# A new opening for a fused attention and MLP kernel: fewer warming products, another load order, another hand-written order up to the table

## The chip, the cores and the metric

The kernel runs on one core of one Trainium2 chip. The metric is device time in microseconds (us) of one execution, as the median of several runs. Five engines work beside each other and wait for one another by semaphores: PE (TensorE, matrix products into PSUM), DVE (VectorE), ACT (ScalarE), POOL (GpSimd) and SP (SyncE, which here only issues DMAs). ACT and POOL issue a few DMAs as well.

## The reference

One sequence of 2048 rows with 576 features goes through a linear-attention block with 32 heads of 18 features and then through an MLP with 4608 hidden units.

```python
qkv = layernorm(x) @ wqkv                 # q, k, v: 32 heads of 18
pq, pk = q @ w_phi, k @ w_phi             # per head, 18 x 18
phi_q = concat(softmax(pq), softmax(-pq)) # 36 features per head
phi_k = concat(softmax(pk), softmax(-pk))
kv  = sum over rows of phi_k * v          # one table per head
z   = sum over rows of phi_k
o   = (phi_q @ kv) / (phi_q @ z + 1e-6)
h   = x + o @ wo
out = h + gelu(layernorm(layernorm(h)) @ w1 + b1) @ w2 + b2
```

No query row can be finished before the table kv has seen all 2048 key rows. So the opening has to produce all keys, values and the table before the first row can go on to the MLP.

## The kernel before, in words

The 2048 rows stand as 16 tiles of 128 partitions, taken in 8 pairs p = 0 to 7. The order of all instructions on all engines is written out by hand: the body ends in a long list of calls, one per step, and each engine carries out its share of the list in that order. A step therefore waits for its own inputs and for whatever stands ahead of it on its engine.

The opening, up to the table, has these parts (lines of the kernel before):

- **Weights.** `warm` (L243) runs products of the identity on PE. `load_wk` (L153) brings the key part of wqkv, `flip_mm`/`flip_ev` (L359, L366) transpose its five chunks on PE and copy them with ACT. w_phi is loaded by two DMAs on POOL (L179, L182) and spread by `spread` (L215) into a block-diagonal form, in five groups on POOL. `fold_k_mm`/`fold_k_ev` (L372, L384) multiply the two into nine blocks of a folded key weight `wkp`. For the queries `load_wq` (L593), `turn_wq` (a DMA transpose, L369) and `fold_mm`/`fold_ev` (L387, L401) do the same later; `swap_q` (L405) copies halves of that weight by DMA.
- **Rows.** `load_x` (L172) brings x; the first two tiles come by ACT's queue (L176). `stats` (L272) takes mean and variance on DVE, `power` (L282) the reciprocal roots on POOL, `scale` (L304) normalises on DVE, or on ACT after `centre` (L297) has made a shift on POOL. A normalised pair is transposed by PE (`turn_x_mm`, `turn_x_ev`, pairs 0 and 1) or by a DMA transpose (`turn_dma`, L318, all other pairs).
- **Products.** `key_mm` and `value_mm` (18 matmuls each, L452 and L427, all by `project` at L416) for each pair and half i of the features; `key_exp` (L455) takes two exponentials on ACT, `value_ev` (L431) copies values with ACT. `key_sum` (L487, on DVE) adds up the softmax sums and takes reciprocals, `key_weigh` (L490) multiplies them in, on POOL but for the last. `query_mm`, `query_exp`, `query_sum`, `query_weigh` do the same for queries.
- **Table.** `sums` (L550) accumulates the table of one tile in the PSUM tile `acc_kv`; `table` (L565) masks it into SBUF. Then `combine_mm` (L627) and `divide` (L648) make attention rows and the MLP begins.

`load_values` (L163) brings the value weights `wv`, as four DMAs: upper half of the partitions by POOL, lower half by SP. PSUM tiles of PE's results in the opening come from one pool, `two`, with three slots (L109), so a product waits until the result three places before it has been copied out. The helper `double_bank` and the tail after the table use the same pool.

Each DMA issued by SP or ACT reuses one of eight semaphore lanes in turn, so an issue waits until the one eight places before it has landed.

## Time and profile before

| | |
|---|---|
| median of 3 runs | 392.47 us (392.47 to 392.67) |
| the profiled execution | 392.93 us |
| span of its trace, first to last instruction | 391.2 us |
| granted TensorE clock | 1.00 |
| read from HBM, written | 17.20 MB, 2.36 MB |

The page of the profile gives busy time by engine, the busy share of forty equal slices of the span, DMA queues, and the chain of work that ended last, followed back from the last instruction. PEld is the load of weights into the array, which overlaps PE. In the timeline a row is: start, duration, engine, line, operation, output<-inputs, count, and in brackets how long the engine had been idle and what released it. A row of several instructions spans them all. An engine with q behind its name is its instruction queue, for example while it issues a DMA. A group row gives busy time and mean ns of one. A DMA row gives size and the median time from issue to landing.

### The profile page before, as it was taken

To read this page: it belongs to the slowest core of one execution; us is meant where nothing else is said; L and a number is where in the kernel's file an instruction comes from. 1 tells how busy PE (TensorE), PEld (TensorE's weight loads), DVE (VectorE), ACT (ScalarE), POOL (GpSimd) and SP (SyncE) were. 2 spreads that over 40 slices of the span, in tenths; PEclk is the share of its full clock that TensorE was granted. 3 is DMA by queue.
4 is the path that set the end of the run, shared out by engine and by line. 5 is a ranking of instruction groups with operands and counts; after the bars stand their busy time and mean duration, and the time that the engine had idled before them with its cause. 6 is when DMAs were issued, how large, how long until landed. Compare 5 with 4: busy or idle time off the path is not lost.

```text
span 391.2 us, 10237 instructions
## 1 busy us (share of the span) xinstructions
PE 382.1 (98%) x4492; PEld 267.4 (68%) x4493; DVE 163.0 (42%) x367; ACT 165.0 (42%) x293; POOL 119.5 (31%) x154
## 2 busy tenths in 40 slices
PE   7899999999999999999999999999999999999997
PEld 3677877779978887844457887444677864447773
DVE  5899778495248388590029322000470000000100
ACT  4988888578501850056650000666300026661000
POOL 6479798215504564144003111000031110000120
PEclk9999999999999999999999999999999999999999
DMA  8999796999555466723005543000051000000000
GB/s 232 212 165 193 161 200 128 216 313 267 176 106 107 91 107 134 107 61 61 0 2 63 90 106 50 14 1 2 2 112 40 17 17 0 2 2 0 17 32 15
DMA packets 74140, 35.43 MB, mean 91 GB/s; under 512 B 62514, under 2 KB 71296, under 8 KB 73968
## 3 DMA queue, kind: packets, MB, share of 16 engines
q1 hardware_dynamic: 73232, 32.47, 41.0%
q0 software_dynamic: 576, 2.01, 2.2%
q8 instruction: 35, 0.57, 0.6%
q10 hardware_dynamic: 288, 0.30, 0.2%
q14 instruction: 9, 0.07, 0.1%
HBM read 17.20 MB, written 2.36 MB: 50 GB/s over the span
## 4 chain that ended last, share of the span: by engine, by line
PE 89%; DMA 4%; DVE 4%; POOL 1%; issue 1%; ACT 1%; POOLq 0%; DVEq 0%
PE po L1183 36%; PE ph L1139 36%; PE pk L422 6%; PE pa L690 5%; PE pv L422 3%; DMA home<-shared 3%; DMA w<-in_A_w_phi_dram 1%; PE pn L641 1%; DVE st L277 1%; PE acc_kv L558 1%; DVE shared L312 1%; DVE ob L655 0%; POOL w L217 0%; PE pW L392 0%; DVE sk L473 0%
## 5 line engine op out<-in xcount | busy, mean ns | idle before, releaser
L1161 ACT ACTIVATE home<-ph,b1col 128x512 bf16<-128x512 f32 (+1 forms) x180 | 98.5, 599 | 169.3 <-PE ph L1139 165.6
L1183 PE MATMUL po<-w,home 128*128 128x288 bf16 (+2 forms) x1151 | 143.2, 286 | 0.1
L1139 PE MATMUL ph<-shared,w 64*128 64x512 bf16 (+2 forms) x1638 | 141.3, 331 | 0.4 <-DVE shared L341 0.4
L1183 PEld LDWEIGHTS <-home 128*128 128x128 bf16 x1152 | 109.3, 98 | 32.2 <-issue 1.8
L1139 PEld LDWEIGHTS <-w 64*128 64x128 bf16 x1638 | 80.2, 94 | 60.4 <-issue 1.3
L1187 DVE TENSOR_TENSOR ot<-po,hb 128x288 bf16<-128x288 f32 (+2 forms) x32 | 14.4, 452 | 106.7 <-PE po L1183 97.1
L1172 POOL TENSOR_TENSOR hb<-xh,b2bc 128x576 f32<-128x576 bf16 x16 | 20.4, 1275 | 104.5 <-DVE ot L1187 103.0
L422 PEld LDWEIGHTS <-home 64*128 64x128 bf16 x864 | 42.5, 94 | 12.5 <-DMA home<-shared 1.9
L508 POOL TENSOR_TENSOR padded<-home,rq 128x540 bf16<-128x540 bf16 x32 | 34.9, 1103 | 37.2 <-DVE rq L500 15.4
L699 DVE TENSOR_TENSOR xh<-pa,xh 128x288 bf16<-128x288 f32 x32 | 13.1, 448 | 70.8 <-PE pa L690 70.8
L253 POOL TENSOR_TENSOR rs<-va,mhalf 128x1 f32<-128x1 f32 x16 | 8.8, 552 | 104.1 <-DVE va L251 104.1
L479 POOL TENSOR_TENSOR phik<-phik,rk 128x576 bf16<-128x576 bf16 x31 | 35.7, 1181 | 4.0 <-DVE rk L475 2.6
L473 DVE TENSOR_REDUCE sk<-phik 128x64 f32<-128x1152 bf16 x16 | 21.2, 1327 | 4.8 <-ACT phik L444 4.8
L444 ACT ACTIVATE home<-pk 128x576 bf16<-128x576 f32 x32 | 18.9, 653 | 8.8 <-PE pk L422 6.7
L499 DVE TENSOR_REDUCE sk<-home 128x64 f32<-128x1152 bf16 x16 | 21.0, 1313 | 0.0
L422 PE MATMUL pk<-shared,home 64*128 64x288 bf16 x288 | 19.3, 283 | 1.1 <-DMA home<-shared 1.0
L444 ACT ACTIVATE phik<-pk 128x576 bf16<-128x576 f32 x32 | 18.5, 650 | 3.5 <-PE pk L422 3.5
L422 PE MATMUL pv<-wv,home 64*128 64x288 bf16 x288 | 19.7, 283 | 0.2 <-DMA wv<-in_A_wqkv_dram 0.2
L422 PE MATMUL pk<-wqp,home 64*128 64x288 bf16 x288 | 19.7, 283 | 0.2 <-ACT home L444 0.2
L654 DVE RECIPROCAL rec<-pn 128x18 f32<-128x18 f32 (+1 forms) x32 | 8.0, 249 | 28.3 <-PE pn L641 28.3
L690 PE MATMUL pa<-wo,shared 64*128 64x288 bf16 x288 | 18.8, 283 | 0.0
L690 PEld LDWEIGHTS <-shared 64*128 64x128 bf16 x288 | 13.9, 94 | 4.3 <-issue 0.5
(80 smaller groups left out, 202.4 us busy)
## 6 DMA issues: line engine op xcount, KB each, us to landing
w<-in_B_w_dram SPq DMA_DIRECT2D x21, 432.0 KB, 8.3
out_dram<-ot SPq DMA_DIRECT2D x15, 144.0 KB, 1.9
xh<-in_A_x_dram SPq DMA_DIRECT2D x3, 576.0 KB, 10.8
wo<-in_A_wo_dram SPq DMA_DIRECT2D x2, 648.0 KB, 6.7
w<-in_B_w_dram POOLq DMA_DIRECT2D x3, 432.0 KB, 10.1
w<-in_A_wqkv_dram SPq DMA_DIRECT2D x4, 157.5 KB, 9.6
w<-in_A_wqkv_dram SPq DMA_DIRECT2D x2, 288.0 KB, 4.7
wqp<-wqp SPq DMA_DIRECT2D x2, 288.0 KB, 3.5
```

What stands on the lines that cost most here:

```text
L422: nc.tensor.matmul(dst[:, a, 0 : hi - lo], lhs[rows, c, :], w[rows, slot, lo:hi], start=(n == 0), stop=(n == KC - 1),)
L444: nc.scalar.activation(rows[:, :, i * HH : (i + 1) * HH, s, :], flight[key, p, i][:, :, 0:HALF].rearrange("p a (h f) -> p a h f", f=DH), A ...
L473: nc.vector.tensor_reduce(sk[:, :, :], part_of(dst, i), AX.X, ALU.add)
L479: eng.tensor_tensor(part, part, flight["r" + key, p, i][:, a, :].rearrange("p (h o) -> p h o", o=1).to_broadcast([P, NH, DH]), ALU.mult,)
L499: nc.vector.tensor_reduce(sk[:, :, :], part_of(phiq[p], i), AX.X, ALU.add)
L508: eng.tensor_tensor(padded[:, a, g0 * P : (g0 + 5) * P].rearrange("p (g k) -> p g k", k=P)[:, :, 0:STEP].rearrange("p g (h f) -> p g h f", ...
L690: nc.tensor.matmul(pa[a], oT[p % 2][rows, c, :], wo[rows, c, cs], start=(c == 0), stop=(c == KC - 1),)
L1139: nc.tensor.matmul(ph[half][:, lo:hi], w1[p_ // 9][rows, c, p_ % 9 * P : (p_ % 9 + 1) * P], ln2T[rows, c, base + lo : base + hi], start=(c ...
L1161: nc.scalar.activation(hidden(m), ph[half][:, 0:width], AF.Gelu_apprx_tanh, bias=b1col[:, m : m + 1], scale=1.0,)
L1172: nc.gpsimd.tensor_tensor(hb[:, :], xh[:, t, :], b2bc[:, :], ALU.add)
L1183: nc.tensor.matmul(po[:, :], hidden(m)[:, i_ * P : (i_ + 1) * P], w2[m // 18][:, m % 18, cs], start=(j == 0), stop=(j == NM - 1),)
L1187: nc.vector.tensor_tensor(ot[:, cs], po[:, :], hb[:, cs], ALU.add)
```

## The change

Six things change.

1. `warm(13)` becomes `warm(10)`.
2. The small part of w_phi (72 rows) is loaded by ACT's queue instead of POOL's.
3. The first key product, `key_mm(0, 0)`, goes through the nine blocks of the contraction in the order in which they were folded (5, 4, 3, 8, 0, 6, 1, 7, 2) instead of 0 to 8.
4. `power(2)` and `power(3)` take two rows of roots each; before, `power(2)` took all four of pairs 2 and 3.
5. `acc_kv` is zeroed by a memset on DVE instead of an activation on ACT, and the ones column of `vals` is set by a call in the list, `ones()`, instead of at the start.
6. The list of steps up to the table is in a new order, and after the table the remaining query products are in another order.

In the new list several `scale` change engine (nine are on ACT instead of five); `load_values` on SP and the two last `load_x` stand ahead of all `load_wq`; the fold order is new; six products instead of seven stand ahead of `key_mm(2, 0)`; three `key_weigh` instead of one are on DVE.

```diff
     for t in range(2):
         nc.scalar.dma_start(xh[:, t, :], x_v[:, t, :])
+    nc.scalar.dma_start(wph[0:72, 4, :], wphi_rows[504:576, :])
...
-    nc.gpsimd.dma_start(wph[0:72, 4, :], wphi_rows[504:576, :])
...
-    nc.scalar.activation(
-        acc_kv[:, :, :].rearrange("p b (r f) -> p (b r) f", f=P),
-        ident[:, :].rearrange("p (o f) -> p o f", o=1).to_broadcast([P, 8, P]),
-        AF.Copy, scale=0.0,
-    )
-    nc.vector.memset(vals[:, :, :, DH], 1.0)
-
-    def spread(g):
+    nc.vector.memset(acc_kv[:, :, :], 0.0)
+
+    def ones():
+        nc.vector.memset(vals[:, :, :, DH], 1.0)
+
+    def spread(g, eng=nc.gpsimd):
...
     def power(p):
-        n = 2 if p < 2 else 4
+        n = 2 if p < 4 else 4
...
+    fold_order = []
+
...
     def fold_k_ev(c, copy):
+        fold_order.append(c)
         copy(wkp[:, c, :], folded_whole("k", c, P))
...
     def key_mm(p, i):
-        features("k", wkp, p, i, PLAIN)
+        features("k", wkp, p, i, PLAIN if p or i else [(c, c) for c in fold_order])
```

The list before, up to `key_mm(2, 0)`, several calls to a line:

```python
warm(13); load_values(1, 1, pool); load_values(0, 1, pool); load_wk(2); load_wk(1); load_wk(0)
load_x(2, 4); load_x(4, 8); spread(4); flip_mm(4); flip_ev(4, act); stats(0, 0); spread(0)
flip_mm(2); flip_mm(3); flip_ev(2, act); flip_mm(1); flip_ev(3, act); flip_ev(1, act)
flip_mm(0); flip_ev(0, act); spread(1); spread(3); spread(2)
fold_k 3, 8, 4; load_wq(4); stats(0, 1); power(0); fold_k 5; load_wq(1); load_x(8, 12); load_wq(3)
stats(1, 0); fold_k 1, 7; stats(1, 1); scale(0, 0, vec); fold_k_mm(0); window_masks()
load_values(0); fold_k_ev(0, act); load_values(1); power(1); centre(1, 1); fold_k_mm(6)
stats(2, 0); fold_k_ev(6, act); scale(0, 1, vec); scale(1, 1, act); turn_x_mm(0); stats(2, 1)
scale(1, 0, vec); stats(3, 0); turn_x_ev(0, 0, act); load_wq(0); turn_x_ev(0, 1, dve)
stats(3, 1); stats(4, 0); fold_k_mm(2); fold_k_ev(2, act); turn_x_mm(1); stats(4, 1); power(2)
centre(3, 1); scale(2, 1, vec); turn_x_ev(1, 0, act); scale(2, 0, vec); stats(5, 0); load_biases()
stats(5, 1); power(4); key_mm(0, 0); turn_x_ev(1, 1, act); key_mm(0, 1); key_mm(1, 0)
key_exp(0, 0); key_exp(0, 1); centre(4, 1); key_exp(1, 0); value_mm(1, 0); value_mm(1, 1)
value_ev(1, 0, act); value_ev(1, 1, act); turn_wq(1); load_wq(2); turn_dma(2); scale(3, 1, act)
key_mm(1, 1); key_exp(1, 1); turn_wq(0); key_sum(0, 1); key_weigh(0, 1, 1, pool)
key_weigh(0, 1, 0, pool); scale(3, 0, vec); value_mm(0, 0); value_ev(0, 0, act); key_mm(2, 0)
...
```

The list after, up to the same step:

```python
load_wk(1); load_wk(2); load_values(0, 1, pool); load_values(1, 1, pool); warm(10); spread(2, pool)
stats(0, 0); spread(1, pool); flip_mm(4); flip_mm(2); load_wk(0); flip_mm(0); load_x(2, 4)
flip_ev(4, act); flip_ev(2, act); load_x(4, 8); flip_ev(0, act); flip_mm(1); flip_ev(1, act)
stats(0, 1); stats(1, 0); spread(4, pool); spread(0, pool); flip_mm(3); flip_ev(3, act)
spread(3, pool); fold_k 5, 4; fold_k_mm(3); load_values(0); power(0); fold_k_ev(3, act); fold_k 8
load_values(1); load_x(8, 12); fold_k 0; stats(1, 1); scale(0, 0, vec); power(1); fold_k 6
load_x(12, 16); fold_k_mm(1); load_wq(4); stats(2, 0); fold_k_ev(1, act); scale(0, 1, vec)
stats(2, 1); turn_x_mm(0); turn_x_ev(0, 0, act); fold_k 7; scale(1, 1, vec); stats(3, 0)
turn_x_ev(0, 1, dve); load_wq(2); scale(1, 0, vec); fold_k_mm(2); stats(3, 1); turn_x_mm(1)
window_masks(); fold_k_ev(2, act); turn_x_ev(1, 0, dve); stats(4, 0); turn_x_ev(1, 1, dve)
power(2); centre(2, 0); load_wq(1); scale(2, 0, act); centre(2, 1); scale(2, 1, act); power(3)
centre(3, 0); turn_dma(2); stats(4, 1); key_mm(0, 0); key_exp(0, 0); key_sum(0, 0)
key_weigh(0, 0, 1, pool); key_mm(0, 1); key_exp(0, 1); stats(5, 0); key_mm(1, 0); key_exp(1, 0)
value_mm(1, 0); value_ev(1, 0, act); key_weigh(0, 0, 0, pool); key_mm(1, 1); scale(3, 1, vec)
key_exp(1, 1); scale(3, 0, act); stats(5, 1); power(4); centre(4, 1); value_mm(0, 0)
value_ev(0, 0, act); load_wq(0); centre(4, 0); key_sum(0, 1); key_sum(1, 1); key_mm(2, 0)
...
```

From there to the table both lists hold the same steps but for those named above. In the new one `load_biases` comes after the second w1 load, and `load_w1(0, 4)`, `load_wo(1)` and `load_w1(0, 5)` come after `turn_q(0)`. Its end up to the first combine is:

```python
...
key_weigh(6, 0, 0, vec); sums(6, 0); key_weigh(5, 1, 0, pool); sums(5, 0); key_weigh(7, 1, 1, pool)
key_weigh(7, 0, 1, vec); sums(7, 1); sums(5, 1); key_weigh(7, 1, 0, pool); key_weigh(7, 0, 0, vec)
sums(7, 0); query_mm(3, 1); query_exp(5, 0); turn_q(0); load_w1(0, 4); load_wo(1); load_w1(0, 5)
table(0); table(1); query_exp(3, 1); query_mm(1, 0); query_exp(1, 0); combine_mm(1, 0, two)
```

## The prediction

> **What bounds the kernel now.** First the page: busy time, slices and the chain that ended last.

> ```profile
> span 391.2 us, 10237 instructions
> PE 382.1 (98%) x4492; PEld 267.4 (68%) x4493; DVE 163.0 (42%) x367; ACT 165.0 (42%) x293; POOL 119.5 (31%) x154
> ...
> PE   7899999999999999999999999999999999999997
> ...
> PE 89%; DMA 4%; DVE 4%; POOL 1%; issue 1%; ACT 1%; POOLq 0%; DVEq 0%
> ```

> PE carries 89% of the chain, and only the first slices are not full. The profiled execution took 392.93 us, 1.73 over its span; the median of the runs shown is 392.47. So I take a difference in the span and put it on the median. Next the view by windows, cut where the chain of waits changes hands: the first key product, the third pair's key product, the last sums, the first `ph`.

> ```profile
> core 0: us, PE busy (x) PEld busy (x) DVE busy (x) ACT busy (x) POOL busy (x), PEclk, DMA share, GB/s
> 0.00:16.92 16.92, 12.94 (x147) 7.78 (x148) 11.03 (x38) 11.80 (x20) 9.84 (x32) 1.00 0.93 228
> 16.92:25.91 8.99, 8.11 (x126) 6.91 (x126) 8.32 (x19) 7.91 (x14) 5.50 (x8) 1.00 1.26 170
> 25.91:70.23 44.32, 44.01 (x797) 35.24 (x799) 35.74 (x50) 35.82 (x62) 39.29 (x39) 1.00 0.93 171
> 70.23:85.37 15.14, 14.13 (x231) 10.98 (x231) 11.07 (x33) 9.81 (x18) 3.09 (x5) 1.00 1.05 258
> 85.37:391.20 305.83, 302.95 (x3195) 206.54 (x3196) 96.85 (x230) 99.63 (x182) 61.78 (x72) 1.00 0.29 61
> ```

> From 16.92 to 70.23 PE is idle for 0.88 + 0.31 = 1.2 us. So only three things can move the end: when the first key product starts, those 1.2 us, and new gaps. The chain of waits gives the unit prices and the one wait of size:

> ```profile
> 19.22 6.65 DMA home<-shared
> ...
> 25.91 1.28 PE pk L422 x18
> ...
> 29.39 2.20 PE pk L422 x36
> ...
> 46.20 1.20 ACT phik L444 x2
> ...
> 68.24 1.99 PE acc_kv L558 x66
> 70.23 1.21 PE pk L422 x18
> ```

> A product of 18 matmuls costs PE 1.10, a `sums` 0.33, the exponential pair of a product ACT 1.20. `turn_dma(2)`, issued at 19.22, landed at 25.87, and `key_mm(2, 0)` waited for it. The timeline of the first 22 us shows what the start waits for:

> ```profile
> 1.41 5.73 PE L247 MATMUL pw<-ident 128*128 128x512 bf16 x13 [1.41 <-POOL ident masks.py:199]
> 1.42 1.08 SPq L158 DMA_DIRECT2D w<-in_A_wqkv_dram  x2
> ...
> 5.04 0.63 SPq L173 DMA_DIRECT2D xh<-in_A_x_dram  x1
> ...
> 6.38 5.85 SPq L165 DMA_DIRECT2D wv<-in_A_wqkv_dram  x2
> ...
> 6.93 1.12 PE L362 MATMUL pX<-ident,w 128*128 128x128 bf16 x15
> ...
> 7.52 3.08 ACT L367 COPY w<-pX 128x640 bf16<-128x640 bf16 x5 [2.98 <-PE pX L362]
> 7.67 0.82 DVE L277 BATCH_NORM_STATS2 st<-xh 128x6 f32<-128x288 bf16 x2 [1.51 <-DMA xh<-in_A_x_dram]
> 7.96 1.73 POOL L217 TENSOR_TENSOR w<-w,mask 72x72 bf16<-72x72 bf16 x5 [2.24 <-DMA w<-in_A_w_phi_dram]
> ...
> 10.55 4.44 ACT L385 CAST shared<-pW 128x576 bf16<-128x576 f32 x8
> ...
> 10.81 0.57 DVE L312 TENSOR_SCALAR shared<-xh,mv,rs 128x576 bf16<-128x576 bf16 x1 [1.16 <-POOL rs L290]
> ...
> 12.27 0.52 DVE L312 TENSOR_SCALAR shared<-xh,mv,rs 128x576 bf16<-128x576 bf16 x1
> ...
> 15.08 0.37 DVE L341 COPY home<-pT 128x512 bf16<-128x512 bf16 x1
> ...
> 16.15 0.72 ACT L385 CAST shared<-pW 128x576 bf16<-128x576 f32 x1
> ...
> 16.92 3.48 PE L422 MATMUL pk<-shared,home 64*128 64x288 bf16 x54 [0.16 <-ACT shared L385]
> ```

> ACT runs without a gap from the first flip's copy (7.52) through eight folded blocks (14.99); the ninth is copied at 16.15, behind a `scale` and a turned copy, and the key product starts as it ends. Beside it DVE waits 1.16 for the roots, which POOL makes only after the spreads, which wait 2.24 for w_phi.

> **The change part by part.** The landings come from the DMA view of the first 30 us and, for the last two rows, of 16 to 18 and 26 to 27 us:

> ```profile
> GB/s 0 0 84 358 154 251 259 339 331 356 370 300 217 204 187 179 210 245 282 310 237 167 186 205 169 175 207 191 29 218 223 302 102 9 241 140 265 114 98 289
> w<-in_A_wqkv_dram SPq DMA_DIRECT2D x2, 288.0 KB, 4.7
> wv<-in_A_wqkv_dram SPq DMA_DIRECT2D x1, 360.0 KB, 13.7
> wv<-in_A_wqkv_dram SPq DMA_DIRECT2D x1, 288.0 KB, 12.4
> xh<-in_A_x_dram SPq DMA_DIRECT2D x3, 576.0 KB, 10.8
> w<-in_A_w_phi_dram POOLq DMA_DIRECT2D x1, 17.7 KB, 4.3
> ...
> w<-in_A_wqkv_dram SPq DMA_DIRECT2D x1, 157.5 KB, 6.1
> ...
> home<-shared SPq DMA_TRANSPOSE x1, 3.0
> ```

> *Warming.* Thirteen products spanned 1.41 to 6.97, 0.43 each; three fewer free PE 1.3 us sooner, at 5.7. But `load_wk(2)` now stands behind `load_wk(1)`: the same 360 KB as before until both are there, and the second of them landed then at 1.42 + 4.7 = 6.1. First flip 6.1 instead of 6.93: 0.83 won. ACT then: first copy 6.7, five flips 3.08 to 9.8, seven blocks at 4.44/8 = 0.555 to 13.7, the turned copy, of a flip's size and so 0.62, to 14.3, two blocks to 15.4, 15.6 with the 0.72 that a lone one takes. The `scale` that stood between them is gone to DVE.

> *w_phi and spreads.* The first spread now needs only the large part, issued behind `ident` at 1.59: landing 1.59 + 4.3 = 5.9 instead of 7.96. Five spreads end at 7.65, the roots of pair 0 near 8.6, no longer last: DVE has stats(1, 1) until 9.66 (x rows 2 to 4 arrive at 7.67 as before). First scale 9.66 instead of 10.81. One scale and one stats repeat at 12.27 - 10.81 = 1.46, so the fourth scale would start at 14.0; a turned copy (0.37) stands before it: it ends at 14.9. The second transpose (nine matmuls, where fifteen flips took 1.12) ends near 15.7. Both paths so give the **first key product at 15.8 instead of 16.92: 1.1 won**.

> *Folded blocks as they come.* Taken at nothing: the first key product uses the PSUM slot that the last folded block leaves, so by the program's waits it cannot begin earlier, whatever block it reads first. Without it the gain would be the same.

> ```profile
> L308 ACT ACTIVATE shared<-xh,nb,rs 128x576 bf16<-128x576 bf16 x5 | 4.4, 882 | 0.0
> ...
> L208 ACT ACTIVATE acc_kv<-ident 128x1024 f32<-128x1024 bf16 x1 | 1.0, 1022 | 0.0
> ```

> These two rows are of the groups by line in the first 85 us.

> *Zeroing and ones.* The zeroing of acc_kv goes from ACT to DVE, where the trace shows none of this shape; taken at ACT's 1.02, bounds nothing and twice that, it lies before 7.67, when DVE waits for x anyhow. The ones move among the key sums, where DVE has 8.6 us free (44.32 - 35.74). A third DMA issue on ACT (0.4) ends long before 6.7.

> *Roots by pairs.* One `power` more on POOL, 1.2, at 11 to 15 us, where POOL was waiting. Four more `scale` on ACT, 0.88 each, 3.5 us in all: two stand before the first exponential (15.6 to 17.4, which the key product's end at 16.9 covers but for 0.5), the others in ACT's 8.5 free us.

> *SP's order and the data queue.* This decides. `load_values` and both large x loads now go ahead of every `load_wq`; `turn_dma(2)` can be issued once ACT has made its two scales, 17.4 instead of 19.22. Ahead of it are wk 648, x 288 + 288 + 576 + 1152, wv 1296, three wq 394, w_phi 20: 4662 KB, 4.77 MB. The slices above (0.75 us each) sum to 4.49 MB at 20.25 and to 4.77 between 21.4 (without the starved slice of 29) and 22.2. Its own tail was 25.87 less the landing of the load before it, a wq issued at 17.4 that took 6.1: 2.4. That makes 23.8 to 24.6. Of the load that gave the low slices (wq in rows of 252 bytes, biases, a `turn_wq`) less is ahead and x12 to x16 in long rows instead, so I take the early end, **23.8**; the bounds are 20.4 (17.4 plus the 3.0 of a later such transpose) and 26.1.

> PE has six products before `key_mm(2, 0)` now, seven before: it arrives at 15.8 + 6.6 = 22.4 and waits 1.4. Like for like: 25.91 - 23.8 - 1.10 = **1.0 won**. So the wait that grows eats most of what the emptied gaps gave.

> *The rest up to the table.* PE was busy 44.01 of 44.32: nothing can be won. POOL weighs 29 key halves for 31, starting earlier; DVE has two more. Seven query products instead of eight stand before the last sums, two instead of one between them and the first `combine_mm`, where they cover the table. I take the gaps as before. After the table the same eight queries remain, in another order: nothing, with 1.2 (one exponential) either way. `load_wo(1)` and the last two parts of w1 go behind `turn_q(0)`, about 62 us; PE wants wo at 76.6 and w1 at 85.4, cover of 8 us and more. The biases wait until about 45 and are wanted at 81.

> **Sum:** -1.0 on the profiled 392.93 is 391.9; on the median **391.5**.

> **The rivals.**
> *1. The data queue is late, slower.* `load_x(8, 12)` now stands behind SP's wv. In the trace wv held SP for 5.85 us, and its first part landed at 6.38 + 13.7 = 20.1. Its 0.66 MB take 3.9 us at that window's 170 GB/s; the two wq loads no longer ahead give back 1.1 at 228. So x8 lands at 5.04 + 10.8 + 2.8 = 18.6. DVE's `stats(4, 0)` wants it at 16.2, and behind it in DVE's order is `turn_x_ev(1, 1)`, for which `key_mm(1, 0)` waits on PE: 1.9 lost there. `turn_dma(2)` has x12 to x16 (1.9 at 310), the wq (2.3 at 170) and its tail of 2.4 still to go after x8, 25.2, and 26.3 if SP is held once more as it was by wv. Past 24.8 (25.91 - 1.10) the change loses; at 26.3 it is +1.5: **394.0**. For it: the queue is full (share 0.93 to 1.26) and x12 is pulled ahead. Against: wv is then mixed with other traffic, at 167 to 207 GB/s, and such rows move at 300 and more early on.

> *2. Nothing is left.* ACT's 1.20 for an exponential pair stands against PE's 1.10, so runs of key and query products with three PSUM slots go at ACT's pace, and the new order has more of them in a row plus the four scales. Ten such products at 0.1 cancel the sum: **392.5**.

> *3. The queue is early.* Landing before 22.4 removes the wait altogether: 1.1 + 0.9 = 2.0, **390.5**. Against: 4.77 MB by 20 us needs 270 GB/s, more than any window above kept.

> *4. The array is still slow at the first key products.* The warming products run at 512 columns in 0.43 us, 1.2 per ns; a key product runs 9 times 288 columns (two halves at once) in 1.10, 2.4 per ns. The granted clock reads 1.00 in both windows, so it does not show this. If half rate reaches 3.4 us into the key products, 1.7 us are lost: **393.2**. Against: flips and folds lie between, and PE has 10 us of work before 15.8. [...]

> **How the numbers follow.** Forecast 391.5 with 45%, rival 1 27%, rival 2 16%, rival 3 7%, rival 4 5%. 0.2% is 0.79 us, about what a measurement of this kernel tells from no change. The forecast's own range, 391.0 to 392.0, is nearly all beyond it, about 40 of its 45; with rival 3 faster is 0.47. Rival 2, the forecast's edge and the mild half of rival 4 make same 0.23; rival 1 and the rest slower 0.30. The range goes from 390.3, leaving out half of rival 3, to 394.2, which holds rivals 1 and 4.

> **What would show it.** Right: the first pX near 6.1, spreads ending before 8, the first `pk` near 15.8, the wait of `pk` on home<-shared near 23.8, and 25.91 to 70.23 repeated a microsecond earlier with PE as full. Wrong: `st` waiting long for xh at 16 us, or `pk` for a DVE copy (rival 1); ACT without gaps while PE has many of 0.1 to 0.2 (rival 2); key products of 2.2 us (rival 4).

## The result, and the profile after

| kernel | median us | runs | lowest to highest |
|---|---|---|---|
| before | 392.48 | 20 | 391.27 to 393.22 |
| after | 395.17 | 20 | 392.79 to 400.02 |

The ratio of after to before is 1.0065, 95% interval [1.005, 1.0079]: slower by 2.6 us by the ratio, 2.7 by the medians. The forecast was 391.5, faster. The runs of after also spread over 7.2 us, those of before over 2.0. Ratios and intervals, here and below, leave out the runs over 1.5% above the fastest of their kernel (one of after, two of e2, one of e9, each with three or four of the half-rate stretches described below), so a ratio need not be the quotient of two medians. The profiled execution of after took 397.76 us, 1.76 over its span; it is one of the slow ends of that spread, which is kept in mind below.

The page of after, with busy times, the slices of PE and its clock, and the chain by engine:

```profile
span 396.0 us, 10229 instructions
...
PE 383.6 (97%) x4490; PEld 268.8 (68%) x4490; DVE 167.2 (42%) x368; ACT 165.8 (42%) x294; POOL 117.4 (30%) x157
...
PE   6699999899999999999999999999999999999997
...
PEclk9689999999999999999999999999999999999999
...
PE 89%; DMA 5%; DVE 3%; ACT 1%; SPq 0%; issue 0%; ACTq 0%; DVEq 0%
```

Two slices of the clock row are below 9; before has none. The view by windows, cut where the clock changes, where the last weighing starts on DVE and where the first product of the table starts:

```profile
core 0: us, PE busy (x) PEld busy (x) DVE busy (x) ACT busy (x) POOL busy (x), PEclk, DMA share, GB/s
0.00:9.00 9.00, 5.10 (x23) 2.19 (x24) 4.14 (x14) 2.76 (x4) 4.77 (x16) 1.00 0.78 226
9.00:12.40 3.40, 3.40 (x55) 3.20 (x53) 1.83 (x6) 2.94 (x6) 1.97 (x6) 0.51 1.03 198
12.40:15.80 3.40, 1.45 (x36) 1.03 (x31) 1.85 (x6) 2.75 (x6) 1.88 (x7) 0.99 1.06 220
15.80:22.70 6.90, 5.81 (x60) 4.39 (x62) 4.62 (x14) 3.49 (x5) 2.55 (x7) 0.51 0.84 186
22.70:67.85 45.15, 44.65 (x776) 37.45 (x774) 41.41 (x66) 40.36 (x69) 37.98 (x43) 1.00 0.91 150
67.85:76.03 8.18, 7.08 (x154) 5.68 (x149) 6.38 (x8) 4.05 (x8) 5.08 (x7) 1.00 1.02 216
76.03:396.00 319.97, 316.14 (x3408) 214.90 (x3408) 106.95 (x258) 109.50 (x200) 63.17 (x75) 1.00 0.32 69
```

PE ran at half rate (PEclk 0.51) from 9.0 to 12.4 and from 15.8 to 22.7, three stretches of 3.4 us. DVE, free for 8.6 us in the comparable stretch of before, is busy for 41.41 of 45.15. From the table's first product on, 319.97 us remain; before had 391.2 - 71.44 = 319.8, so the loss lies wholly ahead of it. The chain of waits says where it ends late:

```profile
5.26 17.62 DMA xh<-in_A_x_dram
...
22.90 0.83 DVE st L275 x2
...
23.96 0.30 DVE home L339
...
24.30 1.28 PE pk L423 x18
...
67.85 4.00 DVE phik L480
...
71.90 1.82 PE acc_kv L559 x55
...
76.03 0.60 PE pn L642 x17
```

Rows of x are counted here in tiles of 128, so rows 8 to 12 are the tiles 8 to 11. They landed at 22.9; behind the statistics that need them stand the turned copy and `key_mm(1, 0)` at 24.30. At the end the sums into acc_kv wait for weighings on DVE. But the start was late already. The timeline of its first 22 us:

```profile
1.42 4.34 PE L245 MATMUL pw<-ident 128*128 128x512 bf16 x10 [1.42 <-POOL ident masks.py:199]
...
5.59 0.72 PE L360 MATMUL pX<-ident,w 128*128 128x128 bf16 x10
...
8.32 1.72 POOL L215 TENSOR_TENSOR w<-w,mask 126x126 bf16<-126x126 bf16 x5 [3.20 <-DMA w<-in_A_w_phi_dram]
...
8.80 1.69 PE L360 MATMUL pX<-ident,w 128*128 128x128 bf16 x15 [2.49 <-DMA w<-in_A_wqkv_dram]
...
10.50 0.82 DVE L275 BATCH_NORM_STATS2 st<-xh 128x6 f32<-128x288 bf16 x2 [4.49 <-DMA xh<-in_A_x_dram]
...
14.44 0.82 DVE L275 BATCH_NORM_STATS2 st<-xh 128x6 f32<-128x288 bf16 x2 [1.52 <-DMA xh<-in_A_x_dram]
...
16.00 1.14 PE L334 MATMUL pT<-ident,shared 128*128 128x128 bf16 x9 [1.97 <-DVE shared L310]
```

The warming products end early and the first flip starts at 5.59. Then everything waits for a load: the last 15 flips 2.49 us for w_k, the spreads 3.20 for w_phi, DVE 4.49 for rows 2 to 4 of x and 1.52 for rows 4 to 8. The first key product starts at 20.36 (its rows: 36 matmuls in 3.45 us, 1.7 for a product instead of 1.10). That is the slow end: in the profiles of e5 and e9 below, with the same loads, it starts at 18.67 and 17.58. The two gaps of PE, 2.49 and 1.97, lie in the stretches just ahead of those at half rate.

### The profile page after: what moved, and what is told of

Its sections match the earlier page's. It is cut to its first block, busy times and chain, and to the rows that moved or that the text cites. A ratio compares the mean times of both kernels' runs of the same rounds, so it can differ in the third digit from the quotient of the medians.

```text
span 396.0 us, 10229 instructions
## 1 busy us (share of the span) xinstructions
PE 383.6 (97%) x4490; PEld 268.8 (68%) x4490; DVE 167.2 (42%) x368; ACT 165.8 (42%) x294; POOL 117.4 (30%) x157
## 4 chain that ended last, share of the span: by engine, by line
PE 89%; DMA 5%; DVE 3%; ACT 1%; SPq 0%; issue 0%; ACTq 0%; DVEq 0%
PE po L1190 36%; PE ph L1146 36%; PE pk L423 6%; DMA xh<-in_A_x_dram 5%; PE pa L691 5%; PE pv L423 4%; PE pn L642 1%; PE acc_kv L559 1%; DVE phik L480 1%; ACT phik L445 1%; ACT home L445 1%; DVE ob L656 0%; PE pW L393 0%; DVE sk L474 0%; SPq L165 0%; PE pT L334 0%
## 5 line engine op out<-in xcount | busy, mean ns | idle before, releaser
L1146 PEld LDWEIGHTS <-w 64*128 64x128 bf16 x1638 | 78.6, 94 | 62.4 <-issue 1.2
L1179 POOL TENSOR_TENSOR hb<-xh,b2bc 128x576 f32<-128x576 bf16 x16 | 20.4, 1274 | 104.6 <-DVE ot L1194 104.6
L423 PEld LDWEIGHTS <-home 64*128 64x128 bf16 x864 | 43.9, 95 | 10.7 <-issue 1.2
L509 POOL TENSOR_TENSOR padded<-home,rq 128x540 bf16<-128x540 bf16 x32 | 34.8, 1102 | 37.4 <-DVE rq L501 15.4
L480 POOL TENSOR_TENSOR phik<-phik,rk 128x576 bf16<-128x576 bf16 x29 | 32.9, 1161 | 7.8 <-DVE rk L476 7.7
L423 PE MATMUL pk<-shared,home 64*128 64x288 bf16 x288 | 20.9, 293 | 0.5 <-DVE home L339 0.5
## 6 DMA issues: line engine op xcount, KB each, us to landing
xh<-in_A_x_dram SPq DMA_DIRECT2D x3, 576.0 KB, 17.0
w<-in_A_wqkv_dram SPq DMA_DIRECT2D x4, 157.5 KB, 10.0
w<-in_A_wqkv_dram SPq DMA_DIRECT2D x2, 288.0 KB, 6.8
wqp<-wqp SPq DMA_DIRECT2D x2, 288.0 KB, 4.7
```

The source lines that it names most:

```text
L423: nc.tensor.matmul(dst[:, a, 0 : hi - lo], lhs[rows, c, :], w[rows, slot, lo:hi], start=(n == 0), stop=(n == KC - 1),)
L480: eng.tensor_tensor(part, part, flight["r" + key, p, i][:, a, :].rearrange("p (h o) -> p h o", o=1).to_broadcast([P, NH, DH]), ALU.mult,)
L509: eng.tensor_tensor(padded[:, a, g0 * P : (g0 + 5) * P].rearrange("p (g k) -> p g k", k=P)[:, :, 0:STEP].rearrange("p g (h f) -> p g h f", ...
L1146: nc.tensor.matmul(ph[half][:, lo:hi], w1[p_ // 9][rows, c, p_ % 9 * P : (p_ % 9 + 1) * P], ln2T[rows, c, base + lo : base + hi], start=(c ...
L1179: nc.gpsimd.tensor_tensor(hb[:, :], xh[:, t, :], b2bc[:, :], ALU.add)
```

## The granted clock, run by run

Every run lists its mean granted clock, and the values of this kernel come in steps: 1.0, 0.996, 0.991, 0.987, 0.983. One step of 0.0043 on a span of 393 us is 1.7 us, half of the 3.4 of the stretches above, and the profiled execution of after, which has three of them, reads 0.987: a step is one stretch at half rate. So the runs can be sorted by their number of half-rate stretches. For after and for experiment e5, whose PE order is the same, together 32 runs:

| stretches at half rate | 0 | 1 | 2 | 3 | 4 |
|---|---|---|---|---|---|
| runs | 5 | 8 | 10 | 7 | 2 |
| median us | 393.17 | 394.77 | 395.25 | 397.01 | 399.34 |

A straight line through the 32 has a slope of 1.13 us a stretch. The 20 runs of after alone have 4, 5, 7, 3 and 1 runs with 0 to 4 stretches, a mean of 1.6. Of the 110 runs of before that stood beside the experiments, 93 had none and 17 had one. That gave the theories.

**Theory:** the new order of the loads opens gaps on PE (on its array, as the texts below also say), and these throttle its clock; that is most of the loss. **Rival A:** the loads cost their own lateness (rows of x, behind values on SP), the clock is a by-product. **Rival B:** DVE, short of time after its late start, is the bound of the opening's end; this was my own first theory after reading the profile of after, and the times did not bear it out.

## The experiments

Of each kernel: median, ratio to before (measured on the same chip, median of before 392.6 to 393.0) and the mean number of half-rate stretches per run. There are six runs of e4, eleven of e11 and twelve of each other experiment.

| kernel | median us | ratio, 95% interval | stretches |
|---|---|---|---|
| after | 395.17 | 1.0065 [1.005, 1.0079] | 1.60 |
| e4 fillers, zeroing later | 396.94 | 1.0102 [1.0073, 1.0131] | 0.83 |
| e6 fillers with zero weights | 393.13 | 1.0021 [1.0003, 1.0039] | 0 |
| e5 ones early | 395.21 | 1.0070 [1.0043, 1.0097] | 2.08 |
| e10 e6 and e5 together | 393.15 | 1.0002 [0.9983, 1.0022] | 0 |
| e9 thirteen warming products | 395.25 | 1.0039 [1.0016, 1.0062] | 1.17 |
| e7 first loads as before | 392.76 | 1.0008 [0.9988, 1.0029] | 0.75 |
| e2 all loads as before | 393.12 | 1.0008 [0.9985, 1.0032] | 1.08 |
| e3 x ahead of values | 393.84 | 1.0037 [1.0015, 1.006] | 0.75 |
| e1 old order, local edits | 393.15 | 1.0015 [0.9998, 1.0032] | 0.58 |
| e8 e2, ones early, fillers | 392.35 | 0.9994 [0.9974, 1.0014] | 0.08 |
| e11 e8, scales first | 393.57 | 1.0017 [1.0, 1.0034] | 0.09 |
| e12 e11, scales on DVE | 393.17 | 1.0026 [1.0, 1.0052] | 0.25 |

### The clock: e4, e6, e5, e10, e9

**e4.** Fillers in PE's gaps; since they write into acc_kv, its zeroing moves behind them.

```
+    keep(8)            # behind flip_mm(2)
+    keep(8)            # ahead of turn_x_mm(0)
+    keep(3)            # ahead of fold_k_mm(2)
-    nc.vector.memset(acc_kv[:, :, :], 0.0)     (at the start)
+    nc.vector.memset(acc_kv[:, :, :], 0.0)     (in ones())
```

> The changed kernel with 19 filler products on the array (identity by identity into acc_kv, which is zeroed after them instead of at the start) in its three long gaps before the first key product: eight before the flips of chunk 0, eight before the first transposes of x, three before the last folded block. Theory (loads are the main loss and the clock is the second): granted clock 1.00 from 3 us on, first two key products 1.1 us each instead of 1.7, first key product at 19 to 20.4, 393.6 to 394.6, that is 0.6 to 1.6 won and before's time not reached. Rival (the clock is the whole loss): 392.5 or less. Rival (half rate costs nothing, since rows 8 to 12 of x land at 22.9 anyway): 395.2 within 0.4 with a clock of 1.00.

It came out slower than after, 396.94, against every line of that. The clock was held (1.00 in every window up to 70 us), and the first key product started at 17.77; but the waits of PE in its first 80 us, and the slice of windows from 70 to 85 us, show a new loss:

```profile
PE acc_kv L563 <- DVE phik L484: 2.1, 1, 2.1
```
```profile
70.00:85.00 15.00, 14.64 (x248) 11.30 (x247) 8.22 (x23) 7.11 (x12) 1.97 (x3) 0.89 1.03 237
```

The zeroing (0.91 us) had gone into DVE's full stretch at 30.87, the last weighing ended at 69.8, PE waited 2.1 for it and, behind that gap, lost a stretch to half rate (0.89). The experiment was spoilt by its own edit, and it made Rival B look right.

**e6.** The same fillers with a zero weight tile: acc_kv stays zero, and its memset stays at the start.

```
+    nc.vector.memset(naught[:, :], 0.0)
     nc.tensor.matmul(acc_kv[...], naught[:, :], wide, start=True, stop=True)
```

> The changed kernel with the 19 fillers of the kernel before it in this study, but with a zero weight tile, so that acc_kv stays zero and its memset stays at the start: the clock is held and VectorE gets nothing more to do than one memset of 128 by 128 in the first 3 us. Theory (VectorE is the bound of the opening, so the array gains nothing that lasts): clock 1.00, first key product earlier than 20.4, and 394.4 to 395.6, the table's first product still after 74. Rival (the clock costs what the array loses by it, 1.7 us and more): 393.6 or less.

393.13, 2.0 us under after, with a clock of 1.00 in 11 of 12 runs and 0.999 in the other. The windows that held the half rate in after:

```profile
9.00:12.40 3.40, 2.71 (x61) 2.10 (x59) 3.07 (x9) 3.34 (x6) 2.83 (x10) 1.00 1.04 241
12.40:15.80 3.40, 3.22 (x43) 1.96 (x37) 2.05 (x7) 2.38 (x6) 1.39 (x4) 1.00 1.06 273
15.80:19.20 3.40, 3.28 (x52) 2.35 (x51) 3.10 (x9) 2.90 (x5) 1.06 (x3) 1.00 1.01 251
19.20:22.70 3.50, 3.50 (x62) 3.26 (x58) 3.26 (x8) 3.50 (x7) 0.10 (x1) 1.00 1.14 100
```

The fillers do no work of the kernel and leave the loads in their late order. With them go 2.0 of the 2.7 us by the medians, 1.7 of the 2.6 by the ratios (1.0065 - 1.0021 on 392.6). So what I had put down as a rival here was right, and "VectorE is the bound, so the array gains nothing that lasts" was wrong.

The profile of after, at the slow end, is not the right partner for that of e6; that of e5 (395.24 us), measured beside it on the same chip, is nearer. The first three key products of e5 and then of e6:

```profile
18.67 5.56 PE L423 MATMUL pk<-shared,home 64*128 64x288 bf16 x54
18.21 3.48 PE L430 MATMUL pk<-shared,home 64*128 64x288 bf16 x54
```

Neither row has a wait in it. They start 0.46 apart and last 2.08 longer in e5, whose half rate ends at 22.95; the first product of the table comes 1.76 later (73.44 against 71.68). One reservation stays: in the three profiles with nineteen fillers (e4, e6, e10) rows 2 to 4 of x land 5.3 to 6.0 us after issue, in the other four with the same first loads (after, e3, e5, e9) 6.5 to 7.9. Whether that is chance was not tried, and if it is not, a part of the fillers' gain is an earlier start.

**e5, e10.** The ones column of vals is set behind the first statistics again, alone and together with the fillers of e6.

```
     stats(0, 0)
+    ones()
...
     scale(4, 0, act)
-    ones()
```

> The changed kernel with one instruction moved: VectorE's memset of the ones column of vals goes back to the opening, behind the first statistics, where VectorE of the changed kernel waits 4.5 us for rows of x; in the changed kernel it stands at 33.9 to 35.7, and 1.76 us of it are shown as idle time in front of a 0.48-us row. Theory (VectorE, without a pause from 22.9 to 71.9, is what the end of the opening waits for): up to 1.9 us of its chain go, 393.4 to 394.4. Rival (the array's half-rate clock and the late first key product are what is lost): 395.2 within 0.4. Rival (the 1.76 us are no cost of the memset but a wait that moves elsewhere): the same 395.2, with a pause of that size somewhere else on VectorE.

> The changed kernel with both of two edits that were run singly: the zero-weight fillers that hold the clock (393.1 alone) and the ones column of vals set early (395.2 alone, nothing won). Theory (with the clock held, VectorE is the bound of the end of the opening, as the profile of the fillers alone has it at 62 to 68 us, and only then its 1.9 us count): 391.7 to 392.7, VectorE's weighing no longer ahead of the products into acc_kv. Rival (VectorE's memset never counts): 393.1 within 0.4.

Neither won anything by the medians: 395.21 against 395.17, and 393.15 against 393.13, outside the expected 393.4 to 394.4 and 391.7 to 392.7. The memset does cost DVE more than its row: in after its row reads

```profile
35.62 0.48 DVE L211 MEMSET vals<- 128x512 bf16 x1 [1.76 <-issue]
```

and about the same 1.75 stands ahead of it wherever it goes (in e8 at 6.29, while DVE waits for x anyway). In the profile of e10 the sums no longer wait for a weighing, as they did for 0.7 in e6. Yet the medians agree within 0.1 us. By the ratios, each to before on its own chip, e10 is 0.7 us better than e6, but the two intervals overlap. So DVE's end shows in single profiles, above all in that of after, where rows 8 to 12 of x were at their latest; it is not what after loses, since e5 wins nothing, and whether it costs up to 0.7 once the clock is held stays open.

**e9.** `warm(13)` for `warm(10)`, nothing else.

> The changed kernel with thirteen warming products again instead of ten, nothing else: one part of the change undone. They end at about 6.9 instead of 5.6 us, while the flips of chunk 0 wait for w_k until 8.8 anyway. Theory (a stretch of 3.4 us in which the array is too little busy is followed by one at half rate, and each such stretch costs some 1.7 us): the stretch at 9.0 to 12.4 stays at full rate in most runs, the later ones do not; mean clock 0.991 to 1.0, 393.5 to 394.6. Rival (late loads alone set the time): 395.2 within 0.4.

395.25, nothing in the median and 1.0 us by the ratio, with intervals that overlap, though the stretches went from 1.6 to 1.2 a run: outside the expected 393.5 to 394.6 and inside the range of the rival. The profiled run kept its rate at 9 to 12.4 us (clock 1.00), as expected, and lost 16.4 to 19.8 (0.51). So thirteen warming products alone do not bring the loss back, and what the three are worth is not settled; the gap ahead of the first key product (12.4 to 15.8 us in after) stays whatever comes before it.

### The loads: e7, e2, e3

**e7.** The first loads in the order of before:

```
-    load_wk(1)
     load_wk(2)
-    load_values(0, 1, pool)
+    load_wk(1)
     load_values(1, 1, pool)
+    load_values(0, 1, pool)
```

> The changed kernel with its first loads alone in the order of before: the 72-KB piece of w_k ahead of the first 288-KB piece on SP, and the two loads of values on POOL's queue in the other order. Theory (the first 288 KB of w_k in front delay w_phi and x 0 to 8; everything behind follows): rows 2 to 4 land at 7.5 to 8.2, rows 4 to 8 at 10.5 to 11.5, key product (0,0) at 15.5 to 17; rows 8 to 12 still land after 19.5, behind SP's values; 393.6 to 394.8. Rival (the spread of the landings is chance, not order): rows 2 to 4 at 8.5 or later, time 395.2 within 0.5.

392.76, 2.4 us under after (2.2 by the ratios) by two swaps of neighbours, and better than the expected 393.6 to 394.8. The DMA view of the first 30 us, of after and then of e7 (KB of one load, median us from issue to landing):

```profile
w<-in_A_wqkv_dram SPq DMA_DIRECT2D x2, 288.0 KB, 6.8
...
xh<-in_A_x_dram ACTq DMA_DIRECT2D x2, 144.0 KB, 3.4
xh<-in_A_x_dram SPq DMA_DIRECT2D x1, 288.0 KB, 7.9
...
w<-in_A_w_phi_dram POOLq DMA_DIRECT2D x1, 17.7 KB, 6.6
```
```profile
w<-in_A_wqkv_dram SPq DMA_DIRECT2D x2, 288.0 KB, 4.8
...
xh<-in_A_x_dram ACTq DMA_DIRECT2D x2, 144.0 KB, 2.4
xh<-in_A_x_dram SPq DMA_DIRECT2D x1, 288.0 KB, 5.1
...
w<-in_A_w_phi_dram POOLq DMA_DIRECT2D x1, 17.7 KB, 4.9
```

For the first two rows and w_phi this is order and not chance; for rows 2 to 4 the ranges overlap, and the 7.9 of after is the longest of all. Over the 14 profiles of this study, the seven with the first loads of before (before, e1, e2, e7, e8, e11, e12) have 4.9 to 5.6 us for rows 2 to 4 of x, 2.4 to 2.7 for the first two rows and 4.1 to 5.0 for w_phi; the seven with those of after have 5.3 to 7.9, 3.2 to 3.6 and 5.6 to 6.6. The first key product of e7 started at 16.60, and rows 8 to 12 of x, still behind SP's values, landed at 17.08 and held DVE for 0.17: the last part of my expectation, a landing after 19.5, was wrong. Not all gaps went: e7 had 0.75 stretches a run, and its runs at a clock of 1.00 have a median of 392.44. Which of the two swaps does it, and why two orders of the same bytes differ, was not tried.

**e2.** All loads of x, w_k, values and w_q back in the order of before, the compute as in after.

```
+    load_values(1, 1, pool); load_values(0, 1, pool)
+    load_wk(2); load_wk(1); load_wk(0); load_x(2, 4); load_x(4, 8)
     ...
+    load_wq(4); load_wq(1); load_x(8, 12); load_wq(2)     (ahead of SP's values)
```

> The changed kernel with its order of compute, and only the loads of x, w_k, values and w_q on SP and POOL back in the order that they had before. Theory (the new load order makes wk, w_phi and x land late): w_phi's large part lands by 6.0, rows 2 to 4 by 8.5, rows 4 to 8 by 11, rows 8 to 12 by 19; first key product at 15.5 to 17 instead of 20.4, key product (1,0) no longer waits for a load, no half-rate stretch after 15.8; 391.0 to 393.0. Rival (the engines' order is at fault: chunks of the fold in the order 5, 4, 3, 8, fewer statistics early): first key product still after 18.5 and 394.5 or more. Rival (VectorE's three weighings at the end of the opening): whatever the start gains, acc_kv waits for them and the time stays above 394.

393.12, just outside the expected 391.0 to 393.0. The landings of x came as expected, and so did the first key product, at 16.19; a stretch from 16.4 to 19.8 stayed at half rate in the profile (clock 0.51), where none was expected. Its five runs without a half-rate stretch have a median of 391.86, its two with three 397.25.

**e3.** Rows 8 to 16 of x ahead of SP's values, the first loads as in after.

```
+    load_x(8, 12)
+    load_x(12, 16)
     fold_k_ev(3, act)
...
+    load_values(0)
+    load_values(1)
     fold_k_mm(0)
```

> The changed kernel with the loads of rows 8 to 12 and 12 to 16 of x put ahead of SP's two loads of values. Theory (the load of rows 8 to 12 queues behind SP's values): it lands at 17 to 18.5 instead of 22.9, key product (1,0) follows the first two at once, about 0.5 to 1.5 us won, 393.5 to 394.7; the first key product stays near 20.4, since w_k and rows 2 to 8 land as late as before. Rival (the DMA engines as a whole are late, not this queue's order): it lands after 20.5 and the time stays at 395.2 within 0.5.

393.84, 1.3 under after (1.1 by the ratios, whose intervals overlap) and inside the expectation; but its profile started the first key product at 16.92, where it was expected near 20.4. Eleven of the twelve runs had no stretch or one. So rival 1 of the prediction has something to it; the stretches went from 1.6 to 0.75 a run, and how the gain divides between the earlier rows and the clock is not shown.

### What is left of the gain: e1, e8, e11, e12

**e1.** The order of before with the local edits alone (ten warming products, w_phi's small part on ACT, roots by pairs, folded blocks as they come, zeroing by DVE).

> The order of before with the local edits of the change alone: ten warming products for thirteen, the small part of w_phi on ACT's queue, roots by pairs up to the fourth, the first key product by folded blocks in the order of their evictions, acc_kv zeroed by VectorE's memset. Theory (the loss sits in the new order of loads, not in the local edits): 391.7 to 392.6, within 0.2% of before; rows of x 8 to 12 land within 1 us of before's time, the granted clock stays 1.00 after the warming, first key product at 16.4 to 17.0. Rival (the local edits themselves cost: three warming products fewer let the clock drop, or the small part of w_phi on ACT delays it): 393.5 or more, and the granted clock shows half-rate stretches after 9 us.

393.15 beside 393.0: no difference that counts, though outside the expected 391.7 to 392.6. Five of its twelve runs had half-rate stretches, 0.58 a run, where five of the 29 runs of before on the same chip had one each (0.17). So some of the local edits, the fewer warming products perhaps, may let the clock drop even with the loads of before; so few runs do not settle it, and which edit it would be was not tried. In its profile the first key product started at 15.72 instead of 16.92, 1.2 earlier, and the chain of waits shows where that went:

```profile
18.73 6.66 DMA home<-shared
25.43 1.30 PE pk L422 x18
```

The third pair's turned rows landed at 25.39; they landed at 25.87 before. 0.5 of the 1.2 us passed this wait, and the rest was given back to it.

**e8.** The loads of e2, the ones of e5 and six zero-weight fillers ahead of the last folded block.

> The changed order of compute with the loads of before, the ones column set early, and six zero-weight fillers before the last folded block to keep the clock. Theory (late loads, ones and clock together are the loss; the order of compute itself gains): clock 1.00 throughout, first key product at 16 to 16.5, table's first product at 68.5 to 70.5, 389.5 to 391.5, under both kernels. Rival (the order of compute is worth nothing without loss): 392.0 to 393.5.

392.35 beside 392.6, interval [0.9974, 1.0014]: no difference that counts, and the rival's range. The chain of waits has the first key product, later than expected, and the table's first product, inside the expectation, at

```profile
17.05 3.48 PE pk L430 x54
...
69.81 0.72 PE pn L649 x22
```

The table starts 1.6 earlier than before's 71.44, and the span of that one execution, 390.2, is 1.0 under before's. The medians differ by 0.25.

**e11, e12.** From e8: DVE makes the scales of the first key product ahead of the statistics of rows 4 to 8 of x, which wait for their load; then the scales of rows 4 and 5 go from ACT to DVE, and one value product ahead of `key_mm(2, 0)`.

```
-    stats(2, 0)                   (ahead of scale(0, 1), likewise stats(2, 1), stats(3, 0))
     scale(1, 0, vec)
+    stats(2, 0)
...
-    scale(2, 0, act); scale(2, 1, act)
+    scale(2, 0, vec); scale(2, 1, vec)                    (e12)
```

> The combination run before (old loads, ones early, fillers; 392.35) with VectorE's order changed: the statistics of rows 4 to 8 of x, which wait for their load until 11.6, go behind the scales that the first key product needs, and three fillers instead of six. Theory (VectorE, in order, holds the first key product's scales behind a load that they don't need): first key product at 14 to 15 instead of 17.05, the array free of gaps from there except for a wait on values or on turned rows of up to 1.5 us; 390.5 to 392.0, faster than both kernels. Rival (the loads of values or VectorE's own sum take the gain back before the table): 392.0 to 393.0.

> The kernel before this one with the two scales of rows 4 and 5 of x taken from ACT, where they held the first exponentials for 2.7 us of waiting for a root and 1.6 us of work, to VectorE behind the next statistics, and with one value product ahead of the third key product. Theory (the order of compute gains what the first key product comes earlier, as long as no in-order queue holds the next link): first exponential at 17.2 instead of 20.1, no wait of the array of more than 0.5 us before 22, table's first product at 68.5 to 70, 390.7 to 391.9, faster than both kernels by 0.2% or more. Rival (loads of values and turned rows hold the array at 20 to 25 whatever the order): 392.2 to 393.2.

The first key product came at 15.91 and 15.65 (14 to 15 was expected of e11), and the time at 393.57 and 393.17: no gain in either. e12 lies in its rival's range, e11 is slower than both of its ranges. In e11 (timeline of ACT) two scales waited for a root in front of the exponentials,

```profile
18.54 1.62 ACT L313 ACTIVATE shared<-xh,nb,rs 128x576 bf16<-128x576 bf16 x2 [2.68 <-POOL nb L305]
20.07 3.33 ACT L452 ACTIVATE phik<-pk 128x576 bf16<-128x576 f32 x6
```

and in e12 (waits of PE in its first 100 us), with those away, the loads came next:

```profile
PE pk L430 <- DMA home<-shared: 0.9, 1, 0.9
PE pv L430 <- DMA wv<-in_A_wqkv_dram: 0.9, 2, 0.5
```

No version beat both kernels.

**What follows.** Holding the clock alone wins 1.7 to 2.0 us (e6), with the reservation made there. What the loads of before add to that, from 393.15 (e10) to 392.35 (e8), is 0.8 by the medians and 0.3 by the ratios, within the intervals. The new order of compute that then remains is not told apart from before. The two causes do not add: two swaps of first loads alone win 2.4 (e7), and the runs of e7 have 0.75 half-rate stretches instead of 1.6, so loads on time leave fewer gaps for the clock. So Rival A's loads are what starts the loss, and the clock is what carries most of it. What stays open: whether DVE's end counts once the clock is held (e10), why single runs at a clock of 1.00 still scatter by 3.5 us (e10, 391.8 to 395.3), and why e8's and e10's profiled spans, 1.0 under before's, do not show as much in their medians.

## Why the prediction was wrong, step by step

- **Warming**: the first flip was to start at 6.1 and started at 5.59. But the step put all five flips into one run, and those of chunk 0 waited until 8.80 for w_k.
- **w_phi, spreads, x: the step that failed.** "x rows 2 to 4 arrive at 7.67 as before", w_phi at 5.9 and the second w_k at 6.1 were landings of the old order of loads carried over to the new one. They were 10.50, 8.32 and, for the w_k of chunk 0, 8.80. For w_k I counted the bytes ahead, found them equal and took an equal landing; for w_phi and x I took the old landing without a count. e7 undoes two swaps of neighbours and lands 1.0 to 2.8 us earlier than after; over seven profiles of each order the middle values differ by 0.8 for the first two rows, 1.4 for rows 2 to 4 and 1.7 for w_phi.
- **First key product**: 15.8 forecast, 20.36 in the profile of after, 17.58 in that of e9 and 18.67 in that of e5. With the loads of before it was 16.60 (e7) and 16.19 (e2): even so the sum was 0.4 to 0.8 early: the statistics of rows 4 to 8 stand between the scales and wait for their load (0.9 in e2). With these out of the way it was 15.91 and 15.65 (e11, e12).
- **Folded blocks, zeroing, roots**: taken at next to nothing, and e1 measures them together, with the other local edits, at 1.0015 [0.9998, 1.0032]. The zeroing took 0.91 (forecast 1.02). The ones cost DVE 1.9 and not their 0.48, without an effect on the medians (e5, e10).
- **turn_dma(2)**: 23.8 forecast; it was issued at 21.57 and landed near 26.8, but `key_mm(2, 0)` came at 28.89 and found it there. The wait which was to eat the gain was not reached. The sum itself was slightly off as well: the slices reach 4.77 MB at 22.3, or at 21.6 without the starved one, so its two ends were 24.0 and 24.7 and the gain 0.8 instead of 1.0.
- **The rest as before**: PE was full from 24.30 to 67.85, 43.55 of 43.55, but the end of the opening went to DVE in the profile of after (1.1 us of waiting for weighings).
- **Rival 1** (27%) saw the place, rows 8 to 12 of x ahead of a turned copy in DVE's order, but priced the landing at 18.6; it was 22.9 in after. Taking it away wins 1.3 by the medians and 1.1 by the ratios (e3), within intervals that overlap.
- **Rival 4** (5%) named the clock, but as a slow start only; the sum itself had no term for it. The 3.4 us of its price stand in no view of before; what the runs showed are half-rate stretches of that length (3.41 us in the clock record of after) behind gaps, from 9.0 and 15.8 on. The trace argument against it, "flips and folds lie between, and PE has 10 us of work before 15.8", was the mistake: that work came with gaps. PE was busy for 27% of 5.6 to 9.0 us and for 43% of 12.4 to 15.8, and the stretch behind each ran at half rate (0.51). The rival with the smallest chance carried most of the 2.6 us: 1.6 stretches a run at 1.1 us each, where one at 1.7 was priced. Its condition was another, though: the array had reached full rate (e5, e7, e9, e2 and after all show it ahead of the drop, a clock of 0.99 to 1.00 in the window) and lost it again.

## What to carry to other kernels

When a change opens gaps on the array ahead of its steady stretch, price the clock as well as the gap: sort the runs by their mean granted clock, and if the times follow its steps, as here with 1.13 us a stretch, hold it with a few zero-weight products in the gaps (2.0 us by the medians in e6) before explaining anything else. The landings of the first loads went here with their order (a middle value of 5.1 us from issue for rows 2 to 4 of x in seven profiles with that of before, of 6.5 in seven with that of after); a table of landings of the old kernel did not carry over, not even for w_k with the same bytes ahead of it (8.80 for a forecast 6.1). A profile of a kernel that scatters can lie at the slow end, as that of after did (397.76 beside a median of 395.17), so its waits are compared with those of several profiles. And an experiment that moves work to hold one thing still (e4) needs a second one in which that work stays (e6).

## What the runs showed of the hardware that was not expected

```profile
5.59:9.00 3.41, 0.92 (x14) 0.75 (x13) 0.38 (x2) 1.29 (x2) 0.68 (x2) 0.99 1.00 305
```

In the profiles where half-rate stretches can be timed, the 3.4 us ahead of a drop had PE busy for 27% and 43% (after), 48% and 47% (e5), 57% (e2), 51% (e7), 56% (e9) and 40% (e4); stretches busy for 70 to 83% (e2, e7, e9) kept full rate behind them. Back at half rate, stretches of 68% (after) and 77% (e5) were followed by another half-rate stretch, those of 94% and more by full rate.

But the busy share alone does not decide. In e11 and e3 the clock reads 1.00 in every window; counted in steps of 3.41 us from 4.34 and 7.14 us on, e11 has stretches busy for 57% and 45%, e3 one of 55%, and none is followed by a drop. The lowest, of e11, has a single wait of 1.89 us in it:

```profile
17.99:21.40 3.41, 1.52 (x26) 1.23 (x22) 3.11 (x12) 2.86 (x5) 1.81 (x6) 1.00 0.17 34
21.41:24.82 3.41, 3.36 (x54) 2.83 (x50) 3.34 (x7) 3.41 (x7) 1.46 (x2) 1.00 1.11 226
```

What else decides is not shown here.

The edges in after, at 9.0, 12.4, 15.8 and 22.6, are 3.4 us apart or twice that (3.41 and 6.83 in its clock record).

Fillers with a zero weight tile held the clock here: e6, e8 and e10 have 35 of 36 runs at 0.999 or 1.00, the other at 0.996.
